# Five expert tiles of 122 token slots against four of 128 and one of 98 that is computed transposed

## The chip, the cores and the metric

The kernel runs on one core of one Trainium2 chip. The metric is the device time of one execution in microseconds (us), median of several runs. The engines of the core are called PE (TensorE, matmuls), PEld (its weight loads), DVE (VectorE), ACT (ScalarE), POOL (GpSimd) and SP (SyncE, which issues DMAs).

## The reference

A thresholded attention block feeds a mixture of experts in which a hash of the token's number picks the expert. All data is float32.

```python
# attention: q, k, v of shape (8, 8, 576, 64)
scores = scale * np.matmul(q, k.transpose(0, 1, 3, 2))
thresh = np.max(scores, axis=-1, keepdims=True) - tau
scores = np.where(scores >= thresh, scores, -1e9)
attn = softmax(scores)
attn_out = np.matmul(attn, v)
...
# bridge: (8, 8, 576, 64) -> (4608 tokens, 512 features)
x = attn_out.transpose(0, 2, 1, 3).reshape(4608, 512)
...
# experts: w1 (8, 512, 1024), w2 (8, 1024, 512)
expert_idx = token_ids * 2654435761 % 8
for e in range(8):
    mask = expert_idx == e
    h = np.maximum(x[mask] @ w1[e], 0.0)
    out[mask] = h @ w2[e]
```

## The kernel before

**Attention.** The first half walks through 32 pairs of heads, each in five steps of query rows (L594). PE makes scores (L211), DVE negates them and finds the maximum (L222), ACT takes the exponential (L236), DVE masks (L247), PE turns the weights (L258) and multiplies them with v (L289). The outputs go to two scratch tensors in memory. The order of all engines is written out by hand, in `manual_schedule` blocks; each engine runs its instructions in that order and waits on semaphores for its inputs.

**Routing.** Between the attention steps, small pieces of work sort the tokens. Every expert has CAP = 610 slots, KT = 5 tiles of TM = 122. Each token gets a slot number, and its own number is scattered into a slot table in memory (two tables, for even and odd columns of tokens). At L484 two DMAs on SP bring the tables back as `gidx` and `gidx_odd`, and DVE takes the minimum (L488). Slot number p * KT + k of an expert becomes row p of tile k. `gidx[:, e, k]` is then the list of 128 token numbers of a tile; a row without a token holds a number out of bounds, which gathers and scatters skip. The experts get between 533 and 599 tokens each, so all of them fit their slots, and the overflow loop at L759 runs no iteration.

**Experts.** For every expert and tile, POOL gathers 128 rows of x into one of ten buffers `xg` (L101). The steps are:

- Turning (`turn_x`, `put_xT`, L704 to L709): four PE transposes of 122 x 128 into a PSUM tile of the pool `ps_x` (two buffers), and one DVE copy into xT. An expert's tiles are turned while the expert before it is in its second product, one tile ahead of each of that one's tiles.
- First product (`gemm1`, L711): eight chunks of 128 hidden features, each of two halves of 305 slots over four blocks of features, with w1 stationary and the tokens moving. ACT and DVE apply the relu in turn, into `h_sb` of shape [128 hidden, 8 chunks, 610 slots].
- Second product (`gemm2`, L727): for a tile, eight matmuls, one for each chunk. The 122 tokens of h are stationary and the 512 columns of w2 move:

```python
nc.tensor.matmul(o_ps[0:rows], lhsT=h_sb[:, fo, kt * rows:kt * rows + rows],
                 rhs=w2_sb[:, fo, :], start=(fo == 0), stop=(fo == FO - 1))
```

- Output: ACT copies the tile from PSUM (pool `ps_o`, two buffers) to one of five buffers `o`, and POOL scatters its rows to the output (L733, L734).

For expert 0 the turning and the first product lie at the end of the attention stage (`early_xT`, L533; `early_h`, L547; `late_h`, L562). There, three of the four feature blocks are multiplied early, between attention's last steps, and the fourth when its gather has landed; DVE adds it and ACT applies the relu (L572, L573).

The loop over experts (L742) issues, for each: the first product, the loads of w1 and gathers for the expert after next, then five times "turn a tile of the next expert, second product of a tile", then the load of w2 for the expert after next.

Of the kernel before, what the change touches and what calls it, by code (L numbers as in the profile page):

```python
# [9 lines left out]
FP32 = mybir.dt.float32  # L10
# [10 lines left out]
def kernel(  # L21
# [12 lines left out]
    nc = tc.nc  # L34

    B, H, D, S = qT.shape
    N, DIN = out.shape
    E, _, F = w1.shape
    P = 128
    HP = H // 2  # L40
    NP = B * HP
    CO = DIN // P
    FO = F // P
# [9 lines left out]

    KT, TM = 5, 122
    CAP = KT * TM
    CH = CAP // 2
    NOV = 32
    NSLOT = -(-(E * CAP + NOV * P) // P) * P  # L60
    BIG = 1 << 20
    assert all((N - (m - 1) * (CAP + 1) - CAP + P - 1) // P + m - 1 <= NOV
               for m in range(1, E + 1) if m * (CAP + 1) <= N)

# [11 lines left out]
    ident = consts.tile([P, P], FP32, name="ident")  # L78
# [11 lines left out]
    gidx = consts.tile([P, E, KT], I32, name="gidx")  # L90
# [4 lines left out]
    xg_bufs = [consts.tile([P, DIN], FP32, name=f"xg_{i}") for i in range(2 * KT)]  # L95
    xT_0 = consts.tile([P, CO, CAP], FP32, name="xT_0")
# [24 lines left out]
    with tc.tile_pool(name="a_q", bufs=1) as a_q, \  # L121
# [350 lines left out]
        def scatters():  # L472

            for c in range(NTC):
                nc.gpsimd.indirect_dma_start(
                    out=slot_dram[c % 2][:, :],
                    out_offset=bass.IndirectOffsetOnAxis(ap=slot_i[:, c:c + 1], axis=0),
                    in_=tok[:, c:c + 1], in_offset=None, bounds_check=NSLOT - 1,
                    oob_is_err=False)
                yield  # L480
            for _ in range(4):
                yield
            for table, dst in zip(slot_dram, (gidx, gidx_odd)):
                nc.sync.dma_start(out=dst[0:TM], in_=table[0:E * CAP].rearrange(  # L484
                    "(e p k) o -> p e (k o)", e=E, k=KT))
            for _ in range(4):
                yield
            nc.vector.tensor_tensor(out=gidx[:], in0=gidx[:], in1=gidx_odd[:], op=ALU.min)  # L488

        nc.sync.dma_start(out=tau_in[:],  # L490
                          in_=bass.AP(tensor=tau.tensor, offset=0, ap=[[0, P], [1, 1]]))
        load_pair(0)
        nc.sync.dma_start(out=tid32[:],
                          in_=bass.AP(tensor=dataclasses.replace(token_ids.tensor,
                                                                 shape=[2 * N], dtype=I32),
                                      offset=0, ap=[[2 * NTC, P], [2, NTC], [1, 2]]))
# [36 lines left out]
        def early_xT(tr, k0, k1, c0, c1):  # L533

            blocks = [(kt, co) for kt in range(k0, k1) for co in range(c0, c1)]
            dst = xT_0[:, c0:c1, k0 * TM:k1 * TM].rearrange("p c (k q) -> p k c q", k=k1 - k0)
            for i, (kt, co) in enumerate(blocks):
                for r, r1 in ((0, 64), (64, TM)):
                    nc.tensor.transpose(tr[:, r // 64, 64 * i:64 * i + r1 - r],
                                        xg_bufs[kt][r:r1, P * co:P * co + P],  # L540
                                        ident[r:r1, r:r1])
            for r, r1 in ((0, 64), (64, TM)):
                src = tr[:, r // 64, 0:64 * len(blocks)].rearrange(
                    "p (k c q) -> p k c q", k=k1 - k0, c=c1 - c0)
                nc.scalar.copy(dst[:, :, :, r:r1], src[:, :, :, 0:r1 - r])

        def early_h():  # L547

# [37 lines left out]
        with tc.manual_schedule():  # L586
# [7 lines left out]
            for n in range(LAST + NS + 1):  # L594
# [15 lines left out]
                q = p - 1  # L610
# [81 lines left out]
    with tc.tile_pool(name="m_x", bufs=1) as m_x, \  # L692
         tc.tile_pool(name="m_o", bufs=1) as m_o, \
         tc.tile_pool(name="ps_x", bufs=2, space=PSUM) as ps_x, \
         tc.tile_pool(name="ps_o", bufs=2, space=PSUM) as ps_o:

        xT_bufs = [xT_0, m_x.tile([P, CO, CAP], FP32, name="xT_1")]
        h_bufs = [h_0, m_x.tile([P, FO, CAP], FP32, name="h_1")]

        o_bufs = [m_o.tile([P, DIN], FP32, name=f"o_{i}") for i in range(KT)]  # L700
        for o_sb in o_bufs:
            nc.vector.memset(o_sb[:], 0.0)

        def put_xT(xg, xT, kt, rows):  # L704
            tr = ps_x.tile([P, CO, P], FP32, name="xT_ps")
            for co in range(CO):
                nc.tensor.transpose(tr[:, co, 0:rows], xg[0:rows, co * P:co * P + P],  # L707
                                    ident[0:rows, 0:rows])
            nc.vector.tensor_copy(xT[:, :, kt * rows:kt * rows + rows], tr[:, :, 0:rows])  # L709

        def gemm1(w1_sb, xT, h_sb, n, width):  # L711
            for fo in range(FO):
                h_ps = ps_sc.tile([P, 2, 512], FP32, name="sc")
                for i in range(n):
                    for co in range(CO):
                        nc.tensor.matmul(h_ps[:, i, 0:width],  # L716
                                         lhsT=w1_sb[:, co, fo * P:fo * P + P],
                                         rhs=xT[:, co, i * width:i * width + width],
                                         start=(co == 0), stop=(co == CO - 1))
                dst = h_sb[:, fo, 0:n * width].rearrange("p (i t) -> p i t", i=n)  # L720
                if fo % 2 == 0:
                    nc.scalar.activation(dst, h_ps[:, 0:n, 0:width], AF.Relu)  # L722
                else:
                    nc.vector.tensor_scalar(out=dst, in0=h_ps[:, 0:n, 0:width], scalar1=0.0,  # L724
                                            scalar2=None, op0=ALU.max)

        def gemm2(w2_sb, h_sb, kt, idx, rows):  # L727
            o_ps = ps_o.tile([P, DIN], FP32, name="o_ps")
            for fo in range(FO):
                nc.tensor.matmul(o_ps[0:rows], lhsT=h_sb[:, fo, kt * rows:kt * rows + rows],  # L730
                                 rhs=w2_sb[:, fo, :], start=(fo == 0), stop=(fo == FO - 1))
            o_sb = o_bufs[kt % len(o_bufs)]
            nc.scalar.copy(o_sb[0:rows], o_ps[0:rows])  # L733
            nc.gpsimd.indirect_dma_start(  # L734
                out=out[:, :], out_offset=bass.IndirectOffsetOnAxis(ap=idx, axis=0),
                in_=o_sb[:], in_offset=None, bounds_check=N - 1, oob_is_err=False)

        def turn_x(e, kt):
            put_xT(xg_bufs[(e * KT + kt) % (2 * KT)], xT_bufs[e % 2], kt, TM)

        with tc.manual_schedule():
            for e in range(E):  # L742
                if e > 0:
                    gemm1(w_tiles.pop((e, 1)), xT_bufs[e % 2], h_bufs[e % 2], 2, CH)
                if e + 2 < E:
                    load_w1(e + 2)
                    for g in range(2 * KT):
                        fetch(e + 2, g // 2, g % 2)
                w2_sb = w_tiles.pop((e, 2))
                for kt in range(KT):  # L750
                    if e + 1 < E:
                        turn_x(e + 1, kt)
                    gemm2(w2_sb, h_bufs[e % 2], kt, gidx[:, e, kt:kt + 1], TM)
                if e + 2 < E:
                    load_w2(e + 2)


        n_ov = nc.values_load(ov_i[0:1, NOV:NOV + 1], min_val=0, max_val=NOV)  # L758
        with tc.For_i(0, n_ov, 1) as it:  # L759
            ex = nc.values_load(ov_i[0:1, bass.ds(it, 1)], engines=[mybir.EngineType.Pool],  # L760
                                min_val=0, max_val=E - 1)
            w1_sb = w_pool.tile([P, CO, F], FP32, name="w1_sb")
            w2_sb = w_pool.tile([P, FO, DIN], FP32, name="w2_sb")
            nc.gpsimd.dma_start(
                out=w1_sb[:],
                in_=w1[bass.ds(ex, 1)].rearrange("o (c p) f -> p (o c) f", p=P))
            nc.gpsimd.dma_start(
                out=w2_sb[:],
                in_=w2[bass.ds(ex, 1)].rearrange("o (c p) d -> p (o c) d", p=P))
            idx = m_o.tile([P, 1], I32, name="idx_ov")  # L770
            idx_odd = m_o.tile([P, 1], I32, name="idx_odd")
            for table, dst in zip(slot_dram, (idx, idx_odd)):
                nc.gpsimd.dma_start(out=dst[:], in_=table[bass.ds(it * P + E * CAP, P), :])
            nc.vector.tensor_tensor(out=idx[:], in0=idx[:], in1=idx_odd[:], op=ALU.min)
            gather(xa_dram, xg_bufs[0][:, 0:XA], idx[:, 0:1])
            gather(xb_dram, xg_bufs[0][:, XA:DIN], idx[:, 0:1])
            put_xT(xg_bufs[0], xT_0, 0, P)
            gemm1(w1_sb, xT_0, h_0, 1, P)
            gemm2(w2_sb, h_0, 0, idx[:, 0:1], P)
# [34 lines left out]
```

## Time and profile before

| what | value |
|---|---|
| time, median of 3 runs | 1031.35 us |
| the runs | 1029.94, 1031.35, 1032.63 us |
| profiled execution, span | 1030.0 us |
| PE busy | 1012.2 us (98%) |
| DVE, ACT, POOL busy | 507.8, 445.7, 316.2 us |
| second product (L730), PE | 640 passes, 280.6 us busy |
| first product (L716), PE | 896 passes, 231.2 us busy |
| turning of gathered tiles (L707), PE | 140 passes, 20.4 us busy |
| copy of an output tile (L733), ACT | 40 of 585 ns |

A row of the profile names line, engine, operation, the tiles written and read, their shapes, how many there were, the busy time in us and the mean ns of one. For weight loads and matmuls "128*122" is the part of the array that is used: rows (contracted) and columns (stationary). A matmul instruction of the program can appear as several passes, each with its own weight load on PEld. Busy times of overlapping passes are counted once, so the busy time divided by the number is closer to the distance between two starts than the mean duration is.

### The profile page before, as it was taken

How to read it: one execution, taken by the hardware profiler on the slowest of the kernel's cores; microseconds unless marked ns; L12 is line 12 of the kernel's file. 1: busy time of each engine (PE TensorE's matmuls, PEld its weight loads, DVE VectorE, ACT ScalarE, POOL GpSimd, SP SyncE). 2: the span in 40 equal slices, each digit the busy share in tenths (PEclk: the TensorE clock that was granted, in tenths of full speed). 3: DMA queues.
4: the chain of work that ended last, by engine and by line, in shares of the span. 5: the costliest groups of instructions: out<-in, count | busy, mean ns of one | idle time of the engine just before them, and what ended most of it. 6: DMA issues, size and time to landing. Idle time of an engine off the chain costs nothing. (4 is left out here: it accounts for less than half of the span.)

```text
span 1030.0 us, 19768 instructions
## 1 busy us (share of the span) xinstructions
PE 1012.2 (98%) x7432; PEld 613.0 (60%) x7432; DVE 507.8 (49%) x1353; ACT 445.7 (43%) x725; POOL 316.2 (31%) x431
## 2 busy tenths in 40 slices
PE   8999999999999999999999999999999999999996
PEld 5666666666666666666547456465475574664752
DVE  7999999999999999973300101101001010010000
ACT  5888888988888988870201000000000000000000
POOL 3233332677763255323423040140130311001001
PEclk9999999999999999999999999999999999999998
DMA  7345554445575867311413242142032312200000
GB/s 177 87 112 135 137 125 120 95 105 113 117 198 142 227 186 172 82 32 31 135 53 113 101 141 63 64 142 91 34 129 101 132 42 91 99 9 28 10 18 28
DMA packets 92019, 103.45 MB, mean 100 GB/s; under 512 B 24589, under 2 KB 65679, under 8 KB 91924
## 3 DMA queue, kind: packets, MB, share of 16 engines
q1 hardware_dynamic: 83300, 83.06, 30.0%
q0 software_dynamic: 8192, 18.91, 5.4%
q8 instruction: 60, 0.98, 0.4%
q14 instruction: 35, 0.29, 0.1%
q10 hardware_dynamic: 432, 0.21, 0.1%
HBM read 81.87 MB, written 20.01 MB: 99 GB/s over the span
## 5 line engine op out<-in xcount | busy, mean ns | idle before, releaser
L730 PE MATMUL o_ps<-w_sb,h 128*122 128x512 f32 x640 | 280.6, 592 | 0.0
L236 ACT ACTIVATE w<-ns,nmx 128x576 f32<-128x576 f32 x288 | 220.3, 776 | 34.7 <-DVE ns L222 34.7
L716 PE MATMUL sc<-xT,w_sb 128*128 128x305 f32 x896 | 231.2, 419 | 0.0
L247 DVE SCALAR_TENSOR_TENSOR w<-ns,thr,w 128x576 f32<-128x576 f32 x288 | 226.0, 817 | 0.0
L222 DVE TENSOR_SCALAR_CACHE_REDUCE ns<-sc 128x576 f32<-128x576 f32 x288 | 205.4, 746 | 5.9 <-PE sc L211 5.2
L716 PEld LDWEIGHTS sc<-xT,w_sb 128*128 128x128 f32 x896 | 169.1, 189 | 63.4 <-issue 3.4
L730 PEld LDWEIGHTS o_ps<-w_sb,h 128*122 128x122 f32 x640 | 115.5, 185 | 138.9 <-issue 138.5
L211 PE MATMUL sc<-k_sb,q 64*128 64x288 f32 (+1 forms) x1280 | 179.0, 423 | 1.3 <-DVE k_sb L517 0.7
L734 POOL DMA_INDIRECT out_dram<-o,gidx x40 | 39.5, 987 | 413.9 <-ACT o L733 400.2
L229 POOL TENSOR_SCALAR thr<-nmx,drop 128x2 f32<-128x2 f32 (+1 forms) x160 | 102.3, 639 | 188.5 <-DVE ns L222 176.5
L258 PEld LDWEIGHTS tr<-ident,w 64*128 64x128 f32 x2624 | 107.2, 139 | 88.6 <-ACT wT_b L279 26.2
L733 ACT COPY o<-o_ps 122x512 f32<-122x512 f32 x40 | 23.4, 585 | 293.5 <-PE o_ps L730 282.4
L724 DVE TENSOR_SCALAR h<-sc 128x610 f32<-128x610 f32 x28 | 22.2, 793 | 256.9 <-PE sc L716 256.9
L258 PE MATMUL tr<-ident,w 64*128 64x64 f32 x2624 | 139.5, 231 | 2.5 <-ACT wT_a L279 2.0
L709 DVE COPY xT<-xT_ps 128x488 f32<-128x488 f32 x35 | 23.3, 665 | 183.4 <-PE xT_ps L707 183.4
L211 PEld LDWEIGHTS sc<-k_sb,q 64*128 64x128 f32 (+1 forms) x1280 | 93.4, 178 | 23.1 <-DVE ns L222 9.3
L289 PE MATMUL av<-wT_a,v 128*64 128x320 f32 (+1 forms) x704 | 100.4, 418 | 0.0
L722 ACT ACTIVATE h<-sc 128x610 f32<-128x610 f32 x28 | 19.0, 679 | 182.7 <-PE sc L716 182.7
L279 ACT COPY wT_a<-tr 128x512 f32<-128x512 f32 (+1 forms) x128 | 81.7, 638 | 20.1 <-PE tr L258 19.6
L279 ACT COPY wT_b<-tr 128x512 f32<-128x512 f32 (+1 forms) x128 | 81.2, 634 | 9.2 <-PE tr L258 6.8
L289 PE MATMUL av<-wT_b,v 128*64 128x256 f32 x640 | 83.2, 389 | 0.0
L289 PEld LDWEIGHTS av<-wT_a,v 128*64 128x64 f32 x704 | 43.8, 137 | 28.5
(99 smaller groups left out, 515.3 us busy)
## 6 DMA issues: line engine op xcount, KB each, us to landing
w_sb<-in_moe_w_dram SPq DMA_DIRECT2D x16, 2048.0 KB
q<-in_q_dram SPq DMA_DIRECT2D x62, 288.0 KB
v<-in_v_dram SPq DMA_DIRECT2D x32, 256.0 KB
xa_scratch<-xm SPq DMA_DIRECT2D x24, 256.0 KB
k_sb<-in_k_dram SPq DMA_DIRECT2D x31, 144.0 KB
k_sb<-in_k_dram SPq DMA_DIRECT2D x32, 112.0 KB
xg<-xg SPq DMA_DIRECT2D x9, 256.0 KB
xb_scratch<-xm SPq DMA_DIRECT2D x8, 256.0 KB
```

Of the source, the lines that this page charges most:

```text
L211: nc.tensor.matmul(sc[out_rows, i, 0:S2], lhsT=q_sb[rows, h, q0:q1], rhs=k_sb[rows, h], start=True, stop=True)
L222: nc.vector.tensor_scalar(out=ns[:].rearrange("p (i s) -> p i s", i=2), in0=sc[:, :, 0:S2], scalar1=-1.0, scalar2=None, op0=ALU.mult, op1= ...
L229: nc.gpsimd.tensor_scalar(out=thr[:, 0:j + 1], in0=stats[n][0][:, 0:j + 1], scalar1=drop[:], scalar2=None, op0=ALU.add)
L236: nc.scalar.activation(w, nss[n, j][:], AF.Exp, bias=stats[n][0][:, j:j + 1], scale=-1.0)
L247: nc.vector.scalar_tensor_tensor(out=w, in0=nss.pop((n, j))[:], scalar=stats[n][1][:, j:j + 1], in1=w, op0=ALU.is_le, op1=ALU.mult, accum_ ...
L258: nc.tensor.transpose(dst[:, r, 64 * c:64 * c + 64], src[rows, c0:c0 + P], ident[rows, rows])
L279: nc.scalar.copy(dst, tr[:, :, 0:64 * n_c].rearrange("p r (c q) -> p r c q", c=n_c))
L289: nc.tensor.matmul(av[64 * j:64 * j + 64, g, c0:c1], lhsT=v_sb[:, c, 64 * j:64 * j + 64], rhs=wT[g][:, i, c0:c1], start=(c == 0), stop=stop)
L716: nc.tensor.matmul(h_ps[:, i, 0:width], lhsT=w1_sb[:, co, fo * P:fo * P + P], rhs=xT[:, co, i * width:i * width + width], start=(co == 0), ...
L730: nc.tensor.matmul(o_ps[0:rows], lhsT=h_sb[:, fo, kt * rows:kt * rows + rows], rhs=w2_sb[:, fo, :], start=(fo == 0), stop=(fo == FO - 1))
L733: nc.scalar.copy(o_sb[0:rows], o_ps[0:rows])
L734: nc.gpsimd.indirect_dma_start(out=out[:, :], out_offset=bass.IndirectOffsetOnAxis(ap=idx, axis=0), in_=o_sb[:], in_offset=None, bounds_ch ...
```

## The change

CAP stays 610, and so do the first product and its halves. The five tiles of an expert have 128, 128, 128, 128 and 98 slots. Everything that turned, gathered or stored 122 rows handles 128 or 98.

The 98-slot tile's second product is made in the transposed form: the blocks of w2 (128 x 128) are stationary, and the 98 tokens of h move. The result is four blocks of [128 features, 98 tokens] beside each other in one PSUM tile. ACT copies it to SBUF, PE turns it with four transposes into [98 tokens, 512 features], and copy and scatter follow as for the others. In the order of the expert loop the transposed product stands first, tile 0 second, the turning back third, and then tiles 1, 2 and 3.

The table of slots is read with four DMAs, two for each table, since rows 98 to 127 have four tiles and the others five. `early_xT` copies the 98-row tile separately.

```diff
-    KT, TM = 5, 122
-    CAP = KT * TM
+    KT, TL = 5, 98
+    TROWS = [P] * (KT - 1) + [TL]
+    CAP = sum(TROWS)
...
-                nc.sync.dma_start(out=dst[0:TM], in_=table[0:E * CAP].rearrange(
-                    "(e p k) o -> p e (k o)", e=E, k=KT))
+                for p0, p1, k in ((0, TL, KT), (TL, P, KT - 1)):
+                    nc.sync.dma_start(
+                        out=dst[p0:p1, :, 0:k],
+                        in_=bass.AP(tensor=table.tensor, offset=p0 * KT,
+                                    ap=[[k, p1 - p0], [CAP, E], [1, k]]))
...
-            for r, r1 in ((0, 64), (64, TM)):
-                src = tr[:, r // 64, 0:64 * len(blocks)].rearrange(
-                    "p (k c q) -> p k c q", k=k1 - k0, c=c1 - c0)
-                nc.scalar.copy(dst[:, :, :, r:r1], src[:, :, :, 0:r1 - r])
+            for ka, kb in ((k0, min(k1, KT - 1)), (max(k0, KT - 1), k1)):
+                for r in (0, 64):
+                    if ka >= kb:
+                        continue
...
+                    nc.scalar.copy(dst[:, :, :, r:r1], src[:, :, :, 0:r1 - r])
...
+        oT_sb = m_o.tile([P, CO * TL], FP32, name="oT_sb")
...
-                nc.tensor.matmul(o_ps[0:rows], lhsT=h_sb[:, fo, kt * rows:kt * rows + rows],
+                nc.tensor.matmul(o_ps[0:rows], lhsT=h_sb[:, fo, kt * P:kt * P + rows],
                                  rhs=w2_sb[:, fo, :], start=(fo == 0), stop=(fo == FO - 1))
+            store(o_ps, kt, idx, rows)
+
+        def gemm2_last(w2_sb, h_sb):
+
+            oT_ps = ps_o.tile([P, DIN], FP32, name="o_ps")
+            for co in range(CO):
+                for fo in range(FO):
+                    nc.tensor.matmul(oT_ps[:, co * TL:co * TL + TL],
+                                     lhsT=w2_sb[:, fo, co * P:co * P + P],
+                                     rhs=h_sb[:, fo, CAP - TL:CAP], start=(fo == 0),
+                                     stop=(fo == FO - 1))
+            nc.scalar.copy(oT_sb[:], oT_ps[:, 0:CO * TL])
+
+        def turn_last(idx):
+            o_ps = ps_x.tile([P, CO, P], FP32, name="xT_ps")
+            for co in range(CO):
+                nc.tensor.transpose(o_ps[0:TL, co, :], oT_sb[:, co * TL:co * TL + TL], ident[:])
+            store(o_ps[:].rearrange("p c d -> p (c d)"), KT - 1, idx, TL)
...
-            put_xT(xg_bufs[(e * KT + kt) % (2 * KT)], xT_bufs[e % 2], kt, TM)
+            put_xT(xg_bufs[(e * KT + kt) % (2 * KT)], xT_bufs[e % 2], kt, TROWS[kt])
...
                     if e + 1 < E:
                         turn_x(e + 1, kt)
-                    gemm2(w2_sb, h_bufs[e % 2], kt, gidx[:, e, kt:kt + 1], TM)
+                    if kt == 0:
+                        gemm2_last(w2_sb, h_bufs[e % 2])
+                        continue
+                    gemm2(w2_sb, h_bufs[e % 2], kt - 1, gidx[:, e, kt - 1:kt], P)
+                    if kt == 1:
+                        turn_last(gidx[:, e, KT - 1:KT])
```

More of the change, by code (lines that the diff above doesn't have):

```diff
@@ L535, in early_xT @@
             blocks = [(kt, co) for kt in range(k0, k1) for co in range(c0, c1)]
-            dst = xT_0[:, c0:c1, k0 * TM:k1 * TM].rearrange("p c (k q) -> p k c q", k=k1 - k0)
             for i, (kt, co) in enumerate(blocks):
-                for r, r1 in ((0, 64), (64, TM)):
+                for r in (0, 64):
+                    r1 = min(r + 64, TROWS[kt])
                     nc.tensor.transpose(tr[:, r // 64, 64 * i:64 * i + r1 - r],
@@ L541, in early_xT @@
                                         ident[r:r1, r:r1])
-            for r, r1 in ((0, 64), (64, TM)):
-                src = tr[:, r // 64, 0:64 * len(blocks)].rearrange(
-                    "p (k c q) -> p k c q", k=k1 - k0, c=c1 - c0)
-                nc.scalar.copy(dst[:, :, :, r:r1], src[:, :, :, 0:r1 - r])
+            for ka, kb in ((k0, min(k1, KT - 1)), (max(k0, KT - 1), k1)):
+                for r in (0, 64):
+                    if ka >= kb:
+                        continue
+                    rows = TROWS[ka]
+                    r1 = min(r + 64, rows)
+                    dst = xT_0[:, c0:c1, ka * P:ka * P + (kb - ka) * rows].rearrange(
+                        "p c (k q) -> p k c q", k=kb - ka)
+                    i0, i1 = (ka - k0) * (c1 - c0), (kb - k0) * (c1 - c0)
+                    src = tr[:, r // 64, 64 * i0:64 * i1].rearrange(
+                        "p (k c q) -> p k c q", k=kb - ka, c=c1 - c0)
+                    nc.scalar.copy(dst[:, :, :, r:r1], src[:, :, :, 0:r1 - r])
         def early_h():
@@ L708, in put_xT @@
                                     ident[0:rows, 0:rows])
-            nc.vector.tensor_copy(xT[:, :, kt * rows:kt * rows + rows], tr[:, :, 0:rows])
+            nc.vector.tensor_copy(xT[:, :, kt * P:kt * P + rows], tr[:, :, 0:rows])
         def gemm1(w1_sb, xT, h_sb, n, width):
@@ L729, in gemm2, with store @@
             for fo in range(FO):
-                nc.tensor.matmul(o_ps[0:rows], lhsT=h_sb[:, fo, kt * rows:kt * rows + rows],
+                nc.tensor.matmul(o_ps[0:rows], lhsT=h_sb[:, fo, kt * P:kt * P + rows],
                                  rhs=w2_sb[:, fo, :], start=(fo == 0), stop=(fo == FO - 1))
+            store(o_ps, kt, idx, rows)
[13 more added lines that the diff above has]
+            store(o_ps[:].rearrange("p c d -> p (c d)"), KT - 1, idx, TL)
+        def store(o_ps, kt, idx, rows):
             o_sb = o_bufs[kt % len(o_bufs)]
```

## The prediction

> **What bounds the kernel now.** I read the page first (busy shares, groups), then the busy times by stage, then the timeline of one pair of token tiles, then two places where weight loads stand close together. A change this small is settled by a few nanoseconds per pass.
>
> ```profile
> PE 1012.2 (98%) x7432; PEld 613.0 (60%) x7432; DVE 507.8 (49%) x1353; ACT 445.7 (43%) x725; POOL 316.2 (31%) x431
> ...
> L730 PE MATMUL o_ps<-w_sb,h 128*122 128x512 f32 x640 | 280.6, 592 | 0.0
> ...
> L716 PE MATMUL sc<-xT,w_sb 128*128 128x305 f32 x896 | 231.2, 419 | 0.0
> L716 PEld LDWEIGHTS sc<-xT,w_sb 128*128 128x128 f32 x896 | 169.1, 189 | 63.4 <-issue 3.4
> L730 PEld LDWEIGHTS o_ps<-w_sb,h 128*122 128x122 f32 x640 | 115.5, 185 | 138.9 <-issue 138.5
> ```
>
> L730 is the second product. 8 experts x 5 tiles x 8 chunks are 320 matmuls, but the row counts 640: a float32 matmul runs as two passes, and each pass has a weight load of its own. 592 ns is how long one pass is in flight; passes overlap, so what counts is the distance between starts.
>
> ```profile
> core 0: us, PE busy (x) PEld busy (x) DVE busy (x) ACT busy (x) POOL busy (x), PEclk, DMA share, GB/s
> 0.00:499.78 499.78, 492.26 (x5756) 312.36 (x5757) 462.04 (x1289) 401.80 (x655) 224.06 (x339) 1.00 0.50 125
> 499.78:1019.60 519.82, 519.82 (x1678) 300.62 (x1676) 45.77 (x65) 43.27 (x69) 91.13 (x92) 1.00 0.23 78
> 1019.60:1030.00 10.40, 0.09 (x1) 0.00 (x0) 0.00 (x0) 0.58 (x1) 0.98 (x1) 0.67 0.06 24
> ```
>
> In the expert stage, where nearly all of the change lies, TensorE is busy for the whole 519.82 us at full granted clock, while DVE, ACT and POOL are busy 46, 43 and 91 us. So every nanosecond added to TensorE's order in this stage moves the end, and copies on ACT cost nothing unless TensorE waits for them. The 10.4 us after it (last copy, scatter) keep their form.
>
> ```profile
> 708.37 7.03 PE L730 MATMUL o_ps<-w_sb,h 128*122 128x512 f32 x16
> ...
> 715.24 0.58 PE L707 MATMUL xT_ps<-ident,xg 122*128 122x122 f32 x4
> 715.24 0.35 PEld L707 LDWEIGHTS xT_ps<-ident,xg 122*128 122x128 f32 x3 [0.29 <-issue]
> ...
> 715.56 0.29 PEld L730 LDWEIGHTS o_ps<-w_sb,h 128*122 128x122 f32 x2
> 715.66 7.03 PE L730 MATMUL o_ps<-w_sb,h 128*122 128x512 f32 x16
> ```
>
> A tile of second product takes 715.24 - 708.37 = 6.87 us, 0.429 per pass of 512 columns; a turn of a gathered tile takes 715.66 - 715.24 = 0.42, 0.104 per transpose. The load line is the important one: two loads of 122 columns are over in 0.29, each lasts 0.185, so the second started 0.105 after the first, when the first pass began. Loads are ahead of their passes by one, and no more.
>
> ```profile
> 464.04 0.81 PEld L554 LDWEIGHTS sc<-xT,w_sb 128*128 128x128 f32 x4 [0.39 <-issue]
> ...
> L568 PE MATMUL sc<-xT,w_sb x32: 417/420/524, 491.3 to 499.8; 128*128 128x305 f32 x32
> ```
>
> Loads of 128 columns: four in 0.81. The last lasts 0.189 and loads two to four keep step with passes of 305 columns, 0.256 apart (starts in the trace; L716's row gives 231.2 / 896 = 0.258), so the first two stand 0.81 - 0.189 - 2 x 0.256 = 0.109 apart. In the second line (duration of L568's passes, minimum, median, maximum) a pass that finds no weights ready lasts 524 ns instead of 420: 104 more, the time in which 128 columns go in. So about 0.105 to 0.109 us for 128 columns, twice.
>
> **What the skill says.** The Trainium skill, "TensorE: Matmul & The Clock Gate", section "LDWEIGHTS (loading the stationary operand)", prices a load by its columns alone, columns / 1.2 ns: 107 ns for 128. The trace agrees (0.105 to 0.109). The same page, "Step-by-step: what each phase is for", says that loads are pulled ahead into a background buffer while a matmul streams; the trace agrees: L716's passes start 0.256 apart although their loads last 189 ns. Its section "Back-to-back issue gap" gives a sustained 81 ns per matmul at 128 columns, for load and matmul pairs; nothing here shows that, and its section "Weight-path perf modes — Fast Weight Load (FWL) and DoubleRow" says that the fast load is not for float32. So I don't use the 81 except for a rival.
>
> **The change part by part**, per expert unless said.
>
> 1. Removed: one of the five tiles of 16 passes. Was 5 x 6.87 = 34.35 us, leaves 4 x 6.87 = 27.48. Stationary blocks of 128 instead of 122 columns don't matter at 0.429 per pass: a load of 0.109 fits under it.
>
> 2. Added: the last tile with w2 stationary: 4 output blocks x 8 chunks x 2 = 64 passes of 98 columns, each behind a load of 128. Streaming 98 columns: from 0.429 at 512 and 0.256 at 305, 0.836 ns per column, hence 0.256 - 207 x 0.000836 = 0.083. Loading takes longer than streaming, so the pass is paced by its load: load i+1 starts when pass i starts, pass i+1 when load i+1 is in. I take 0.1085: 64 x 0.1085 = 6.94 us. The tile of 98 rows thus costs as much as a tile of 122 did. Low end 0.107 (the skill's price, no handover): 6.85. High end 0.110: 7.04.
>
> 3. Added: turning the output back, 4 transposes with 128 identity columns moving: L707's 0.104 for 122 scaled, 0.109 each, 0.44 us. They wait for ACT's copy of 128x392, which is issued when the 64 passes end and needs under 0.6 (L733's 128x512-sized copy: 585 ns); a whole tile of 6.87 us stands between. The PSUM slot they take was emptied by DVE (0.67) a tile before. Hidden: 0.
>
> 4. Turning the next expert's tiles: 16 transposes of 128 and 4 of 98 instead of 20 of 122: 16 x 0.109 + 4 x 0.083 - 20 x 0.104 = 0.0.
>
> 5. The new first consumer of h. The 98-column tile needs chunk 7 after 14 passes, 1.5 us after the second product begins, where it was 6.0. Experts 1 to 6: DVE's relu of chunk 7 started 0.45 after the last pass of the first product started and took 0.79 (708.15 to 708.94 in the trace); chunk 7 is needed at about 708.37 + 1.5 = 709.9. Expert 7, without a turn ahead, keeps about 0.4 us. Expert 0: ACT's last relu runs from 501.05 to 501.76, needed at 500.45 + 14 x 0.1085 = 501.97: it just fits. 0, up to +0.3 once for the whole kernel.
>
> 6. ACT gets one copy of 128x392 and, in early_xT, two small ones more (its copies take 0.37 to 0.50). The late ones start at 488.24 and must be done by 491.3, where the first L568 pass starts: four copies take about 1.6. Hidden under L554's passes: 0.
>
> 7. Slot table loads: four DMAs on SP instead of two, 1024 short rows per table instead of 976. Before, the two were issued by 331.4 and landed at about 331.8; DVE's minimum at 340.37 is the next that needs them, behind it on DVE are the masks and maxima that TensorE waits for. 8.6 us of slack against some 0.5 for 5% more rows; even a second 8.8 us (the second issue's time on SP) would only eat the slack. Key loads queued behind them on SP are for two head pairs later (29 us). 0, at most +0.2. POOL has as many gathers and scatters as before; the extra order (tile 4's scatter close behind tile 0's) meets a buffer of its own, and TensorE waits for none.
>
> Sum: 27.48 + 6.94 + 0.44 = 34.86 against 34.35: +0.51 per expert, x 8 = **+4.1 us** (ends +3.4 to +4.9). The profiled span 1030.0 becomes 1034.1. The timed runs before are 1029.94 to 1032.63, median 1031.35, and the profiled run lies inside them; so 1035.4. A difference under 0.3% (3.1 us) can't be told from none here: "slower" starts at 1034.4, "faster" ends at 1028.3.
>
> **Rivals.**
>
> Faster: the load doesn't pace, and a pass costs its 98 columns, 0.083. 64 x 0.083 = 5.31, +0.44, against 6.87: -1.12 per expert, -8.9, 1022.4. For it: the idea that only streamed columns count holds in every 305- and 512-column row of this trace, the skill's 81 ns, and the transposes of 64 rows, whose loads come far closer than 0.1. Against it: the two measured distances of float32 loads that aren't transposes. The break-even is (6.87 - 0.44) / 64 = 0.1005 per pass; over 0.3% faster needs 0.094. 8%.
>
> Slower by a handover: each nanosecond on top of the load's time, where load and pass alternate with nothing to hide behind, costs 512 passes x 1 ns = 0.5 us. Nothing here shows a long run in which loads pace. At 0.118, +9, 1040.3. Against: both close pairs show 0 to 2 ns. 10%.
>
> Much slower: a load must be over (189 ns) before its pass. 64 x 0.19 = 12.2, +46, 1077. Against: the pass at 715.66 started 0.10 after its load began. 3%.
>
> The change doesn't do what it says: the capacity stays 610 slots per expert and the first product is the same, so no work falls away elsewhere.
>
> **How the numbers follow.** Main case 79%, its own range 1033.4 to 1037.0 with the spread of runs; about a sixth of it falls under 1034.4. With handover (10%) and full load (3%): slower 0.79, same 0.13, faster 0.08. Range 1033.0 to 1040.5: it leaves out the faster rival, the 3%, and the tails.
>
> **What would show it.** The row of the new matmuls should have 512 passes, spaced 0.107 to 0.110, with weight loads back to back (TensorE's load row gaining about 512 x 0.107), and the stretch of the 64 passes 6.9 to 7.0 us. A tile of 512-column passes should still be 6.87. The attention stage should end where it did, at about 499.8 within 0.3. Spacing near 0.083 would prove me wrong and make it faster; idle time before the new row put down to ACT or DVE h would show item 5 wrong; idle time at the 98-row transposes, item 3.

## The result, and the profile after

The changed kernel took 1037.91 us (median of 4 runs, 1036.86 to 1038.08), the kernel before beside it 1031.99 (1029.94 to 1032.67): a ratio of 1.0059, 95% interval 1.0041 to 1.0076. It is slower by 5.9 us, where +4.1 was forecast; 1037.91 lies in the stated range (1033.0 to 1040.5, centre 1035.4). A later repeat gave 1.0050 (1.0036 to 1.0065).

The busy times by stage first. The stretches are the attention stage, the expert stage, and what follows the last matmul.

```profile
core 0: us, PE busy (x) PEld busy (x) DVE busy (x) ACT busy (x) POOL busy (x), PEclk, DMA share, GB/s
0.00:499.63 499.63, 492.02 (x5756) 311.66 (x5757) 462.32 (x1289) 402.24 (x657) 224.32 (x339) 1.00 0.50 125
499.63:1025.18 525.55, 525.55 (x2094) 340.19 (x2092) 45.79 (x65) 46.44 (x77) 91.06 (x91) 1.00 0.22 78
1025.18:1035.20 10.02, 0.00 (x1) 0.00 (x0) 0.00 (x0) 0.59 (x1) 0.98 (x1) 0.64 0.06 24
```

The expert stage grew from about 520 us to 525.5, with PE busy in all of it as before: no idle time was added. From the first transpose of expert 1's tiles (500.03 before, 499.88 after) to the end of the last pass (1019.69, 1025.18) it is 519.66 and 525.31, so +5.65; "the stage" below means this stretch. ACT's busy time there grew by 3 us, which nobody waits for.

The groups of matmuls and weight loads, shapes kept apart:

```profile
L744 PE MATMUL o_ps<-w_sb,h 128*128 128x512 f32 x512 | 224.9, 593 | 0.0
...
L753 PE MATMUL o_ps<-h,w_sb 128*128 128x98 f32 x512 | 58.3, 275 | 0.0
...
L762 PE MATMUL xT_ps<-ident,oT_sb 128*98 128x128 f32 x32 | 4.8, 273 | 0.0
```

```profile
L744 PEld LDWEIGHTS o_ps<-w_sb,h 128*128 128x128 f32 x512 | 94.9, 190 | 108.1 <-issue 108.1
...
L753 PEld LDWEIGHTS o_ps<-h,w_sb 128*128 128x128 f32 x512 | 57.9, 192 | 0.1
```

L753 is the transposed product. Its passes keep PE busy for 58.3 us over 512, and its loads keep PEld busy for 57.9, with 0.1 us idle between them: the loads follow each other without a gap. L744's loads, which lie under passes of 512 columns, leave 108.1 us idle. The 275 ns of an L753 pass contain waiting: the few that find their weights ready (the first of each group) last 246 to 250. In the trace the next load starts 27 or 28 ns after the recorded start of a pass, which is as much as the pass lasts longer.

One expert on the timeline:

```profile
710.25 7.22 PEld L753 LDWEIGHTS o_ps<-h,w_sb 128*128 128x128 f32 x64
710.35 7.29 PE L753 MATMUL o_ps<-h,w_sb 128*128 128x98 f32 x64
...
717.47 0.60 PE L721 MATMUL xT_ps<-ident,xg 128*128 128x128 f32 x4
717.73 0.49 ACT L757 COPY oT_sb<-o_ps 128x392 f32<-128x392 f32 x1 [11.04 <-PE o_ps L753]
...
717.91 7.03 PE L744 MATMUL o_ps<-w_sb,h 128*128 128x512 f32 x16
...
724.78 0.60 PE L762 MATMUL xT_ps<-ident,oT_sb 128*98 128x128 f32 x4
```

From the first L753 pass to the next transpose it is 717.47 - 710.35 = 7.12 us, where the removed tile took 6.87. ACT's copy is over at 718.22, 6.5 us before the turning back at 724.78. The starts in the trace give these means, and the differences over the stage (rows are rounded):

| | before | after | difference over 8 experts |
|---|---|---|---|
| 16 passes of 512 columns | 6.87 us, 40 of them | 6.88 us, 32 of them | -54.7 |
| 64 passes of 98 columns | | 7.12 us, 8 of them | +57.0 |
| turning back | | 0.44 us, 8 of them | +3.5 |
| turning the next expert's tiles | 14.65 us in all | 14.58 us in all | -0.1 |
| sum | | | +5.65 |

### The profile page after: what moved, and what is told of

Same layout as the page of the kernel before. It is cut to its first block, busy times and chain, and to the rows that moved or that the text cites. A ratio compares the mean times of both kernels' runs of the same rounds, so it can differ in the third digit from the quotient of the medians.

```text
span 1035.2 us, 20626 instructions
## 1 busy us (share of the span) xinstructions
PE 1017.6 (98%) x7848; PEld 651.9 (63%) x7848; DVE 508.1 (49%) x1353; ACT 449.3 (43%) x735; POOL 316.4 (31%) x431
## 5 line engine op out<-in xcount | busy, mean ns | idle before, releaser
L744 PE MATMUL o_ps<-w_sb,h 128*128 128x512 f32 x512 | 224.9, 593 | 0.0
L744 PEld LDWEIGHTS o_ps<-w_sb,h 128*128 128x128 f32 x512 | 94.9, 190 | 108.1 <-issue 108.1
L260 PEld LDWEIGHTS tr<-ident,w 64*128 64x128 f32 x2624 | 106.7, 139 | 88.6 <-ACT wT_b L281 25.8
L723 DVE COPY xT<-xT_ps 128x512 f32<-128x512 f32 (+1 forms) x35 | 23.3, 665 | 187.4 <-PE xT_ps L721 187.4
L767 ACT COPY o<-o_ps 128x512 f32<-128x512 f32 x32 | 18.8, 586 | 213.1 <-PE o_ps L744 166.8
```

What stands on the lines that cost most here:

```text
L260: nc.tensor.transpose(dst[:, r, 64 * c:64 * c + 64], src[rows, c0:c0 + P], ident[rows, rows])
L723: nc.vector.tensor_copy(xT[:, :, kt * P:kt * P + rows], tr[:, :, 0:rows])
L744: nc.tensor.matmul(o_ps[0:rows], lhsT=h_sb[:, fo, kt * P:kt * P + rows], rhs=w2_sb[:, fo, :], start=(fo == 0), stop=(fo == FO - 1))
```

## The experiments

The experiments ran on three chips on which the kernel before takes 1.3 to 1.6% longer than it did beside the first result. Their traces show pauses of PE of several us, and a halved clock for 7 to 14 us, at the end of the attention stage. So each is compared by its ratio to the kernel before on the same chip, and by its rows in the expert stage. The changed kernel's stage is 525.31 us in both of its traces.

**The sizes alone.** The transposed product is put back to the old form:

```diff
-                    if kt == 0:
-                        gemm2_last(w2_sb, h_bufs[e % 2])
-                        continue
-                    gemm2(w2_sb, h_bufs[e % 2], kt - 1, gidx[:, e, kt - 1:kt], P)
-                    if kt == 1:
-                        turn_last(gidx[:, e, KT - 1:KT])
+                    t = (kt - 1) % KT
+                    gemm2(w2_sb, h_bufs[e % 2], t, gidx[:, e, t:t + 1], TROWS[t])
```

> The sizes 128, 128, 128, 128, 98 alone: the last tile's second product in the old form (its 98 tokens stationary, 512 columns of w2 moving, 16 passes), issued first in each expert as in the changed kernel, no turning back. Theory (the loads of the transposed tile pace it): everything the change cost goes away. Five tiles of 16 passes at 0.429 to 0.430 are 34.4 us per expert as before, so within 0.3% of the kernel before, near 1032. Rival (sizes, slot table reads, small copies or the new order cost part of it): slower than before by 2 us or more.

```profile
L744 PE MATMUL o_ps<-w_sb,h 128*98 128x512 f32 x128 | 56.2, 592 | 0.0
```

Measured: ratio 0.9997 (0.9987 to 1.0008), and a stage of 519.75 us against 519.66 in the kernel before. A tile of 98 stationary tokens takes 6.87 us, one of 128 takes 6.88. The sizes, the four slot table reads, the copies in `early_xT` and the new order together cost nothing that shows; the loss is the transposed form.

**Half of the tokens moving.** Here and in the next cuts the dots stand for the output slice and ACT's copy, which follow the new size.

```diff
...
-                                     rhs=h_sb[:, fo, CAP - TL:CAP], start=(fo == 0),
+                                     rhs=h_sb[:, fo, CAP - TL:CAP - TL // 2], start=(fo == 0),
...
```

> The changed kernel with 49 instead of 98 tokens moving in the transposed product; the other 49 tokens of the last tile are left out of the second product. Theory (a pass waits for its weight load): spacing stays 111 to 112 ns and the 64 passes 7.12 us, so 1037.9 within 1 us. Rival 1 (streamed columns plus a fixed 28 ns per pass): spacing falls by 49 x 0.836 = 41 ns, 512 passes, -21 us, 1017. Rival 2 (the 2.8 ns by which the measured spacing exceeds my 108.5 come from streaming beside the load): spacing 108.5, -1.4 us.

Measured: 1070.72 and 1073.41 us at a mean clock of 0.97, 1088.38 and 1088.45 at one of 0.96, against 1048.04 for the kernel before. Even the lowest is 2% slower, which no theory had expected. The row of the passes, and two stretches of one group in the busy times by stretch:

```profile
L754 PE MATMUL o_ps<-h,w_sb 128*128 128x49 f32 x512 | 67.9, 300 | 0.0
```

```profile
590.40:594.90 4.50, 4.50 (x43) 4.50 (x41) 1.20 (x2) 0.00 (x0) 0.00 (x0) 1.00 0.79 246
596.00:599.40 3.40, 3.40 (x18) 3.40 (x18) 0.00 (x0) 0.00 (x0) 0.00 (x0) 0.50 0.39 159
```

The column after the busy times is PEclk: 1.00 in the first stretch, 0.50 in the second. In the first, starts of passes are 111 to 113 ns apart, as with 98 tokens. So rival 1 (columns plus a fixed price: 70 ns) falls, and so does rival 2 (108.5): streaming half as much beside the load changes nothing. In the second stretch the spacing is 213 ns. The granted clock is halved in all eight groups, 3.7 to 6.6 us after the group's first pass, and stays so for 3.4 to 10.2 us, past the end of the group. The stage is 546.68 us, 21.4 more than the changed kernel's; 9.4 of them lie in the groups, 12.0 in the transposes and 512-column tiles that follow at the halved clock. Half the streaming made the kernel slower, through the clock.

**Fewer columns to load.** 96 of each 128 columns of w2:

```diff
-                    nc.tensor.matmul(oT_ps[:, co * TL:co * TL + TL],
-                                     lhsT=w2_sb[:, fo, co * P:co * P + P],
+                    nc.tensor.matmul(oT_ps[0:96, co * TL:co * TL + TL],
+                                     lhsT=w2_sb[:, fo, co * P:co * P + 96],
...
```

> The changed kernel with 96 of each 128 columns of w2 loaded in the transposed product; a quarter of the last tile's output features is left out. Theory (the load paces, 0.833 ns per column and about 5 ns): a load is 85 ns, as long as the 98 columns stream, so spacing 85 to 87, -13 us against the changed kernel, near 1025. Rival 1 (streamed columns plus a fixed 28 ns): no change, 1037.9. Rival 2 (a load has a price that doesn't depend on its columns): no change, 1037.9.

```profile
L754 PE MATMUL o_ps<-h,w_sb 128*96 128x98 f32 x512 | 45.1, 248 | 0.0
```

Measured: ratio 0.9925 (0.9911 to 0.9939), so 1.3% under the 1.005 of the changed kernel's repeat, 13 us; the stage is 512.10 us, 13.2 less. The spacing is 85 ns, a group of 64 takes 5.47 us, and the mean duration is back at 248: the passes no longer wait. Both rivals, which expected no change, fall.

**More tokens moving.** 128 tokens, to fill the part of the load's time that 98 leave free:

```diff
...
-                                     rhs=h_sb[:, fo, CAP - TL:CAP], start=(fo == 0),
+                                     rhs=h_sb[:, fo, CAP - P:CAP], start=(fo == 0),
...
```

> The changed kernel with 128 instead of 98 tokens moving in the transposed product (30 of them belong to tile 3 and their result is thrown away). Theory: 128 columns stream in 109 ns, still under the load's 111.7, so the spacing stays 111 to 113 ns, the 64 passes 7.1 to 7.2 us, and the ratio to before stays at 1.006. Rival (columns plus a fixed 28 ns): spacing 137, +13 us against the changed kernel, ratio 1.018.

```profile
L753 PE MATMUL o_ps<-h,w_sb 128*128 128x128 f32 x512 | 58.5, 275 | 0.0
```

Measured: 58.5 us busy against 58.3, 7.15 us per group, spacing 111.7; ratio 1.0050 (1.0035 to 1.0065), the same as the changed kernel's repeat. 30 more tokens cost nothing: 98 tokens, which stream in some 83 of the load's 112 ns, leave a quarter of it unused.

**The load's price at another size, and the clock.** Two kernels, one run each. The first loads 64 columns and moves 49 tokens, the second loads 128 and moves 73 (the diffs are as above, with other numbers).

> The changed kernel with half of the columns of w2 loaded and half of the tokens moving in the transposed product (three quarters of the last tile's second product are left out). It measures the load's price at a second size: theory 0.833 ns per column and 5 ns fixed, 58 ns at 64 columns, above the 43 ns that 49 columns stream. Rival 1 (the price is proportional, 0.872 ns per column): 56. Rival 2 (a large fixed part): over 70. If the granted clock falls with the share of time in which columns stream, it stays full here (43 of 58 is 73%, as 82 of 112 in the changed kernel), where it fell to half in the run with 128 columns loaded and 49 moving (41 of 112).

> The changed kernel with 73 tokens moving in the transposed product (25 left out). Spacing stays 111 to 112 ns at full clock by the load theory. It asks how far the streaming share of a pass may fall before the granted clock is halved: 61 of 112 ns is 55%, between the changed kernel's 73% (full clock) and the 37% of the run with 49 moving (halved after some 4.7 us). If about half is the limit, the clock stays full and the time is that of the changed kernel; if not, the last passes of each group stand 213 ns apart and the kernel loses 10 us or more.

```profile
L754 PE MATMUL o_ps<-h,w_sb 128*64 128x49 f32 x512 | 31.8, 223 | 0.2 <-ACT h L586 0.2
```

```profile
L754 PE MATMUL o_ps<-h,w_sb 128*128 128x73 f32 x512 | 58.1, 274 | 0.0
```

The first: nearly all starts are 58 or 59 ns apart. With 111.7 at 128 columns that is (111.7 - 58.3) / 64 = 0.834 ns per column and 4.9 ns fixed, as theory said; a proportional price (56) falls short by 2. This line has only two points: at 96 columns it gives 85 and 85 was measured, but there the stream takes as long. The clock is full in the groups, but they are over after 3.9 us, and in the run with 128 by 49 the clock had fallen by then in only one group of eight: this run can't tell whether the streaming share matters. The 0.2 us of waiting for h is expert 0's chunk 7, which these faster passes reach too soon: the spare time of step 5 is as narrow as computed. Its time was 1027.96 us in one run. The second: starts 111 and 112 apart, clock full in the groups, which last 7.1 us, and a stage of 525.17 us; 1051.49 us in one run (before: 1048.24). So with 61 of 112 ns streaming the clock stays, and with 41 of 112 it is halved.

**Two tiles transposed together.** If a pass costs the greater of load and stream, then the transposed form pays where the stream is the longer. Three tiles in the old form, 226 tokens in the other:

```diff
+        KN = 3
+        M0 = KN * P
+        MT = CAP - M0
...
-                                     lhsT=w2_sb[:, fo, co * P:co * P + P],
-                                     rhs=h_sb[:, fo, CAP - TL:CAP], start=(fo == 0),
+                nc.tensor.matmul(oT_ps[:, i, 0:MT], lhsT=w2_sb[:, fo, co * P:co * P + P],
+                                     rhs=h_sb[:, fo, M0:CAP], start=(fo == 0),
...
+                    if kt < 2:
+                        gemm2_last(w2_sb, h_bufs[e % 2], kt)
+                        continue
+                    gemm2(w2_sb, h_bufs[e % 2], kt - 2, gidx[:, e, kt - 2:kt - 1], P)
+                    if kt < 4:
+                        turn_last(kt + 1, gidx[:, e, kt + 1:kt + 2])
```

The product is made in two halves (two blocks of output features each), into the PSUM tiles that the first product leaves free.

> The transposed form for the last two tiles together: three tiles of 128 in the old form, and 226 tokens (128 and 98) moving against standing w2, turned back with eight transposes. Theory: a pass of 226 columns streams for 226 x 0.836 + 2 = 191 ns, its load of 112 is hidden, so 64 x 191 = 12.25, + 8 x 0.109 = 13.12 us per expert against two tiles of 6.87 = 13.74: -0.62 x 8 = -5.0 us against the kernel before, near 1027, and -11 against the changed one. Rival (28 ns per pass on top of the columns, whatever their number): 64 x 219 = 14.0 + 0.87 = 14.9, +9 us against before, near 1041.

```profile
L747 PE MATMUL o_ps<-w_sb,h 128*128 128x512 f32 x384 | 168.9, 593 | 0.0
L757 PE MATMUL sc<-h,w_sb 128*128 128x226 f32 x512 | 100.2, 353 | 0.0
L767 PE MATMUL xT_ps<-ident,oT_sb 128*98 128x128 f32 x32 | 4.8, 273 | 0.0
L767 PE MATMUL xT_ps<-ident,oT_sb 128*128 128x128 f32 x32 | 4.8, 273 | 0.0
```

Measured: ratio 0.9950 (0.9937 to 0.9963), 1043.37 us against 1048.04. By the ratios it is 0.5% faster than the kernel before and 1% faster than the changed one. The stage is 514.61 us, 5.05 less than before, where -5.0 was expected. 64 passes take 12.22 us (spacing 191), no idle time appears, and the rival with a fixed price per pass falls.

**Three tiles transposed together**, the same with KN = 2: 354 tokens, three tiles turned back one after the other behind tile 0.

> The transposed form for the last three tiles together: two tiles of 128 in the old form, 354 tokens moving against standing w2, turned back with twelve transposes. Theory (the greater of load, 112 ns, and stream sets a pass): 64 passes of 354 x 0.836 + 2 = 298 ns are 19.07, + 12 x 0.109 = 20.38 us per expert against three tiles of 6.87 = 20.61: -0.23 x 8 = -1.8 us against the kernel before, ratio 0.998, so 226 columns stay the better cut. Rival (28 ns per pass on top of the columns): +12 us, ratio 1.012.

Measured: ratio 1.0055 (1.0034 to 1.0075): a miss, slower where theory said 0.998. The passes are as expected (297.6 ns, 19.05 us per expert). What theory had left out stands in two other rows. First the turning back, then POOL's scatters of the last expert on the timeline:

```profile
L767 PE MATMUL xT_ps<-ident,oT_sb 128*98 128x128 f32 x32 | 5.1, 283 | 2.7 <-ACT o L772 2.7
```

```profile
1030.83 0.97 POOL L773 DMA_INDIRECT out_dram<-o,gidx  x1 [52.88 <-ACT o L772]
...
1034.23 0.98 POOL L773 DMA_INDIRECT out_dram<-o,gidx  x1 [2.43 <-DMA out_dram<-o,gidx]
1037.65 0.97 POOL L773 DMA_INDIRECT out_dram<-o,gidx  x1 [2.44 <-DMA out_dram<-o,gidx]
1038.69 0.59 ACT L772 COPY o<-o_ps 128x512 f32<-128x512 f32 x1 [6.28 <-PE o_ps L747]
1041.11 0.97 POOL L773 DMA_INDIRECT out_dram<-o,gidx  x1 [2.49 <-DMA out_dram<-o,gidx]
1044.47 0.97 POOL L773 DMA_INDIRECT out_dram<-o,gidx  x1 [2.38 <-DMA out_dram<-o,gidx]
```

Three tiles in a row need three PSUM slots where there are two, so PE waits for ACT's copies: 1.86 us per expert for the turning instead of 1.31. That alone makes an expert 19.05 + 1.86 + 2 x 6.88 = 34.67 us against 34.35; with the turning of the next expert's tiles, which is slower by 0.3 us in all, the stage is 522.55 us, 2.9 more than before. And each scatter waits until the one before has landed, 3.4 us from start to start. Four outputs are ready at once behind tile 0, so the last scatter starts at 1044.47, though its data left PSUM at 1039.3; after PE's last pass it takes 14.9 us to the end instead of 10.3. These two, +2.9 and +4.6 us, are of the size of the difference (6.5 us between the medians). That they are the cause was read from the trace, not tested by another order.

**The changed kernel again**, without an edit.

> The changed kernel itself once more, to have it beside the experiments' chips, where all kernels take 1.6% longer. Theory: the loss lies in the expert stage alone and doesn't depend on the chip: +5.6 us, ratio 1.005 to 1.006, the 64 passes 7.12 us and the four that turn back 0.44. Rival (part of the first measured ratio 1.0059 was the chip or the draw of runs): ratio under 1.004.

Measured: ratio 1.0050 (1.0036 to 1.0065), 7.12 us for the 64 passes, 0.44 for the turning back. The rows are those of the first trace to within a nanosecond, though the end of the attention stage differs.

## Why the prediction was right

The mechanism held: the pass of 98 columns is paced by its load of 128, and the tile in the new form is dearer than the one that it replaces. The size was forecast too small: 1037.91 lies above the main case's own range (1033.4 to 1037.0), and the stage's +5.65 above its high end of +4.9. The stated range holds the result because it kept room for the slower rival. Of the 2.5 us between 1035.4 and 1037.91, the stage accounts for 1.55, and 0.64 is the kernel before, which took 1031.99 beside the result instead of 1031.35. By its steps:

1. The removed tile: 6.87 us each, as in the trace; a tile of 128 stationary columns takes 6.88, 0.2 us over 32 of them that were not counted.
2. The 64 passes: **the term that was mis-sized**. 0.1085 per pass was forecast, 0.107 to 0.110 as bounds; 0.1113 was measured as the mean, 111.7 ns in the steady run. That is 7.12 us instead of 6.94, 8 x 0.18 = 1.4 of the 1.55 us by which the stage's +5.65 exceeds +4.1. I had taken the distance between a pair of loads in which the first had nothing ahead of it (0.109), and the price by columns that the Trainium skill gives (107 ns in "TensorE: Matmul & The Clock Gate", section "LDWEIGHTS (loading the stationary operand)"). I had also read a line wrongly: the pair 0.105 apart were loads of 122 columns, not 128. At the skill's price 122 columns make an estimated 102 ns, so the two pairs show 3 and 2 ns on top of their columns, not the "0 to 2" that I held against a handover; and 0.105 scaled to 128 columns is 0.110, the high end. In a run of loads some 5 ns come on top of the columns, at 64 columns as at 128, and whether 128, 98, 73 or 49 tokens stream beside 128 loaded columns. Why a run has 2 to 3 ns more than a pair stays open. In size it is a small form of the slower rival (a handover, 3 ns over my 108.5 where the rival had 10); that it is a handover was not tested.
3. Turning back: 0.437 us against 0.44; ACT's copy and the PSUM slot were hidden as argued.
4. Turning the next expert's tiles: -0.1 us against 0.0.
5. The earlier need for h: no idle time before L753. For expert 0 the relu ended at 501.61, needed at 500.31 + 14 x 0.1117 = 501.87.
6. and 7. ACT's smaller copies, the slot tables: the attention stage ended 0.15 us earlier than before, the four issues were over at 329.2, and DVE's minimum ran at 340.2. The kernel with the sizes alone, ratio 0.9997, shows these at nothing together.

Of the rivals, the faster one (0.083 per pass, -8.9 us) fell with the spacing of 111.7 and with 128 moving tokens at the same price. The one that waits for the whole recorded load (189 ns) fell too.

## What to carry to other kernels

Exchanging the stationary and the moving operand changes what paces a pass: write down both times, load and stream, and take the greater one; at full clock this held in all eight combinations of loaded and moving columns run here. With a stream of 0.836 ns per column and 2 ns, 128 loaded columns of float32 (111.7 ns) cost as much as an estimated 131 moving ones. So the exchange lost with 98 tokens. It won with 226: the load was hidden, and 64 passes of 226 columns stream less than the 32 passes of 512 that they replace, which cost the same however few tokens a tile holds (6.87 us with 98 or 122, 6.88 with 128). And a distance read from two neighbouring loads was 3 ns too short here for a run of hundreds, which is small until it is multiplied by 512.

## What the runs showed of the hardware that was not expected

The granted clock fell although TensorE was never idle. With PE busy without a gap, passes of 49 columns (41 ns) behind loads of 112 ns brought the clock to 0.50 in each of eight groups, 3.7 to 6.6 us after the group began, and for at least 3.4 us. Passes of 73 columns (61 of 112 ns), in groups of 7.1 us, did not. If it is the share of streaming that counts, the limit lies between 37% and 55%; that it is this share was not tested apart from the number of columns, and each side is one kernel's trace. In the half-clock stretches the spacing was 213 ns, twice 106.7, so the fixed 5 ns were not seen there.
